# Four early loads of batch 0 issued by the scalar queue instead of the sync queue

## The chip, the core and the metric

The kernel runs on one core of a Trainium2 chip. The metric is the time of one execution on the device, in microseconds (us); smaller is better. Engines go by the short names of the profile: PE (TensorE, matmuls), PEld (its weight loads), DVE (VectorE), ACT (ScalarE), POOL (GpSimd) and SP (SyncE, which here only issues transfers). A name with a q behind it (SPq, ACTq, POOLq) is the instruction queue of that engine while it issues a transfer.

## What is computed

Attention with a forget gate, for 8 batches, 8 heads, 576 tokens and a head size of 64, is followed by a gated feed-forward layer over all 4608 tokens.

```
scores = q @ k.T / 8;  cum = cumsum(log(clip(f, 1e-4, 1)))
attn   = softmax(where(causal, -1e9, scores + cum[:, None] - cum[None, :]))
x      = (attn @ v)  with the heads side by side        # 4608 x 512
xn     = x / sqrt(mean(x*x) + 1e-6) * rms_g
out    = (silu(xn @ w_gate) * (xn @ w_val)) @ w_out     # 512 -> 1536 -> 512
```

All inputs and the output are float32 in device memory; the matmuls take bf16.

## The kernel before

**Work.** Batches are taken one after the other. For each, q, k and v are loaded as float32 into staging tiles `st` (a pool of 10), q and k are cast to bf16 (`ld`, a pool of 6) and turned so that the head dimension lies on partitions (tiles `QK`, and `QT` for the last 64 tokens). For batch 0 the turning is done by PE against an identity and a copy out of PSUM. Scores go to PSUM (L671), their exponentials to `PT` (L680, ACT), v is multiplied by the decay of its token and stored as `Vs` (L449 to L456), and values (L708), normalisation and the feed-forward layer follow (L857, L883), in groups of tokens that are mixed into the attention of later batches.

**Order.** Nothing is scheduled at run time. Each piece of work has a name, and the string ORDER (L22 to L102) lists all pieces; they are recorded in that order, so each engine's instruction queue has its own pieces in the order of the string. A suffix `@A`, `@D`, `@O` or `@S` puts a piece on ACT, DVE, POOL or SP instead of its default; `*48` puts that much filler matmul work ahead of a PE piece (L250); `:ff` picks a PSUM pool. The engines run their queues in order and meet by semaphores.

**The loads of batch 0.** Every load of q, k and v is issued by SP (`nc.sync.dma_start`). `Lk0.u` and `Lq0.u` load four heads and 256 tokens each (L459), 256 KB. `Lqk00` and `Lqk01` load the last 64 tokens of q and of k (L425), 128 KB each, into the lower and the upper 64 partitions of one staging tile. `Lv0.j` loads 128 tokens of v (L417), 256 KB in rows of 256 bytes; `Lv0.40` and `Lv0.41` load the last 64 tokens of v, the even and the odd heads (L429), 64 KB each. The one transfer that ACT issues early is `lf`, the forget gate (L272). The weights `wg0` to `wv3` (L382) and `wo` (L394) are issued by POOL.

SP's order in the first microseconds is Lk1.0, Lk0.0, Lk0.1, Lq0.0, Lq0.1, Lqk00, Lqk01, Lv0.40, Lk0.2, Lk0.3, Lq0.3, Lq0.2, Lv0.41, Lv0.1, Lv0.2, Lv0.0, Lv0.3, Lk1.2. Transfers of SP and ACT use eight completion semaphores in turn, so in the built program a transfer also waits for the landing of the one eight places before it in the order of the string.

**Who uses them.** ACT's order at the start is lf, fetch_ln (a table load and a small activation, L333), log (L280, needs clip on DVE, which needs lf), fetch (a second table load, L330), Cq0.0, Ck0.1 (casts, L223), expo (L292, needs the scan on DVE), keeptr0.02.k, keeptrt0, esc0.1.0 and so on. The first real work of PE is `tr0.01` (L535), which needs Ck0.0 on DVE and Cq0.0 on ACT; then come turn_rg, far0.1.0 and far0.3.0 (L659), eight units of filler, tr0.02 and tr0.03 (need Ck0.1 and Cq0.1), turn_dec (L302, needs expo and twice), trt0 (L553, needs Cqk0) and the first scores. On DVE, Cq0.1 and Cqk0 (both L223) stand behind twice (L295), which needs expo. POOL's order is Ck0.2, k4.0 (a copy that needs keeptrt0), Ck0.3, Cq0.2, Sv0.1, then the issues of the weights.

Of the kernel before, what the change touches and what calls it, by code (L numbers as in the profile page):

```python
# [11 lines left out]
ACT = mybir.ActivationFunctionType  # L12
PSUM = bass.MemoryType.PSUM

B, H, S, D = 8, 8, 576, 64
# [4 lines left out]
NP = H // 2  # L20

ORDER = """  # L22
one lf tri Lk1.0 Lk0.0 Lk0.1 far Lq0.0 ident Lq0.1 rg identb Lqk00 fetch_ln clip Lqk01 clear Lv0.40 log Lk0.2 Lk0.3 fetch Ck0.0@D scan Lq0.3 Lq0.2
Cq0.0@A Ck0.1@A Lv0.41 tr0.01*48 turn_rg far0.1.0 keeptr0.01.k@D expo Lv0.1 far0.3.0 keeptr0.01.q twice Cq0.1@D Cqk0@D tr0.02*8 Lv0.2 tr0.03
keeptr0.02.k@A keeptr0.02.q turn_dec Ck0.2@O keep_rgT keeptr0.03.k trt0 keeptr0.03.q sc0.1.0 keeptrt0@A keep_dec tr0.00 Lv0.0 esc0.1.0 sc0.3.0 k4.0
keeptr0.00.k far0.0.0*3 keeptr0.00.q@A Ck0.3@O Lv0.3 spread_rg Cq0.3@A Cq0.2 esc0.3.0 Sv0.4 tr0.10 Lk1.2 sc0.0.0 Lqk10 Sv0.1@O far0.2.0 esc0.0.0
keeptr0.10.k@D sc0.2.0 Lq1.2 esc0.2.0 Lq1.0 sc0.1.384*1 Sv0.2 tr0.12 wv1 esc0.1.384 Lqk11 sc4.0 keeptr0.12.k keeptr0.12.q Lk1.1 wg0 exp4.0 sc0.2.384*6
Lk1.3 keeptr0.10.q far0.3.1024 esc0.2.384 mask4.0 sc0.3.1024 Sv0.0 Lq1.1 far0.1.1024 wg1 esc0.3.1024 wv0 sc0.3.384*8 sc0.1.1024 esc0.3.384 wg2
val0.6.0 esc0.1.1024 Lq1.3 sc0.1.512 val0.0.0:ff wv2 val0.2.0:ff xpo0.0.0 esc0.1.512 sc0.2.512 Ck1.0 xpo0.2.0 val0.4.0:ff esc0.2.512 Sv0.3@O xpo0.6.0
# [76 lines left out]
ROWS, RUNS, HALF, TAIL, V4 = (1.2, 26, 64), (0.75, 46, 16), (0.9, 28, 32), (0.64, 24, 32), (0.34, 24, 16)  # L106
# [80 lines left out]
def kernel(  # L187
# [12 lines left out]
    nc = tc.nc  # L200
# [3 lines left out]
    def pool(name, bufs, **kw):  # L204
# [22 lines left out]
    ident = consts.tile([128, 128], BF16, name="ident")  # L227
    tri = consts.tile([128, 64], BF16, name="tri")
# [38 lines left out]
    clear = plan.add("clear", "DVE", 1.75, clear_early)  # L267
# [6 lines left out]
    lf = plan.add("lf", "ACT", 0.65, load_f, xfer=(0.4, 84, 4), acq=[("pt", "pre")])  # L274
# [39 lines left out]
    far = consts.tile([128, 256], BF16, name="far")  # L314
# [91 lines left out]
    def attention(b):  # L406
        i = b % 2
        old, new = hist.get(b - 2, {}), hist.setdefault(b, {})
        split, pe = b in SPLIT, b in PE_TURN
        cold = COLD if b == 0 else 1  # L410

        def stage(key):
            if key not in T:
                T[key] = stp.tile([128, H * D], F32, name="st", tag="st")
            return T[key]

        def load_rows(nm, src, j):  # L417
            nc.sync.dma_start(out=stage((nm + "s", b, j)).rearrange("p (h d) -> p h d", d=D),
                              in_=src[b, :, j * 128:(j + 1) * 128, :].rearrange("h p d -> p h d"))

        def load_runs(nm, src, pp):
            nc.sync.dma_start(out=stage((nm + "s", b, pp)).rearrange("p (h c) -> p h c", h=2),  # L422
                              in_=src[b, 2 * pp:2 * pp + 2, 0:512, :].rearrange("h (p i) d -> p h (i d)", i=4))

        def load_tail(t, src):  # L425
            nc.sync.dma_start(out=stage(("qks", b))[t * 64:t * 64 + 64, :].rearrange("p (h d) -> p h d", d=D),  # L426
                              in_=src[b, :, 512:576, :].rearrange("h p d -> p h d"))

        def load_v4(par):  # L429
            nc.sync.dma_start(out=stage(("vs", b, 4))[par * 64:par * 64 + 64, 0:NP * D].rearrange("p (h d) -> p h d", d=D),  # L430
                              in_=v[b, par::2, 512:576, :].rearrange("h p d -> p h d"))

        def cast(src, dst, eng, runs=False):
# [22 lines left out]
                e.tensor_copy(Vs[i][rows, 4, par::2, D], dj)  # L456

        ld, lv, sv, tq = {}, {}, {}, {}
        def load_half(nm, src, u):  # L459
            hh, z = divmod(u, 2)  # L460
            nc.sync.dma_start(out=stage((nm + "s", b, u)).rearrange("p (h c) -> p h c", h=4),
                              in_=src[b, 4 * z:4 * z + 4, hh * 256:hh * 256 + 256, :].rearrange("h (p i) d -> p h (i d)", i=2))

        def load_qk(us):
            for u in us:
                for nm, src in (("k", k), ("q", q)):
                    key = f"{nm}{b}.{u}"
                    if split:
                        a = [plan.add("L" + key, "SP", 0.65, lambda nm=nm, src=src, u=u: load_half(nm, src, u), xfer=HALF,
                                      acq=[("st", "s" + key)])]  # L470
                        eng = SPLIT_CAST[u][nm]
                    else:
                        fn = load_runs if pe else load_rows
                        a = [plan.add("L" + key, "SP", 0.6 if pe else 0.66, lambda fn=fn, nm=nm, src=src, u=u: fn(nm, src, u),
                                      xfer=RUNS if pe else ROWS, acq=[("st", "s" + key)])]
                        eng = CAST_ON.get((nm, b, u), "POOL")
                    eng = on("C" + key, eng)
                    ld[nm, u] = plan.add("C" + key, eng, {"DVE": 0.45, "ACT": 0.6, "POOL": 0.62}[eng],
                                         lambda nm=nm, u=u, eng=eng: cast((nm + "s", b, u), (nm, b, u), eng, pe), a,
                                         acq=[("ld", key)], rel=["s" + key])  # L480

        def load_tails():
            key = f"qk{b}"
            a = [plan.add(f"L{key}{t}", "SP", 0.66, lambda t=t, src=src: load_tail(t, src), xfer=TAIL,
                          acq=[("st", "s" + key)])
                 for t, src in enumerate((q, k))]
            eng = on("C" + key, "POOL")
            ld["t"] = plan.add("C" + key, eng, 0.62, lambda: cast(("qks", b), ("qk", b), eng), a,
                               acq=[("ld", key)], rel=["s" + key])

        def load_v(js):
            for j in js:
                key = f"v{b}.{j}"
                if j < 4:
                    lv[j] = [plan.add("L" + key, "SP", 0.66, lambda j=j: load_rows("v", v, j), acq=[("st", "s" + key)],
                                      xfer=ROWS)]
                else:
                    lv[j] = [plan.add(f"L{key}{par}", "SP", 0.66, lambda par=par: load_v4(par),
                                      acq=[("st", "s" + key)], xfer=V4) for par in range(2)]
                eng = on("S" + key, "DVE" if b == 0 else SV_ON.get((b, j), "POOL"))  # L500
                sv[j] = plan.add("S" + key, eng, (0.82 if j < 2 else 1.0 if j < 4 else 1.6) if eng == "DVE" else 1.25 if j < 4 else 1.7, lambda j=j, eng=eng: scale_v(j, eng),
                                 lv[j] + [p_dec, clear] + old.get("val", []), rel=["s" + key])
# [12 lines left out]
        if pe:  # L515
# [444 lines left out]
```

## Time and profile before

| | |
|---|---|
| median of 6 runs | 384.1 us (383.68 to 384.99) |
| the profiled execution | 384.56 us |
| its span, first to last instruction | 382.8 us |
| outside the span | 1.8 us |
| PE busy | 369.2 us, 96% of the span |
| DVE, ACT, POOL busy | 265.8, 220.4, 127.3 us |
| transfers issued by SP (q1) | 40.00 MB, 52.8% of 16 DMA engines |
| transfers issued by POOL (q0) | 8.79 MB, 10.8% |
| transfers issued by ACT (q10) | 3.29 MB, 2.5% |

The page cuts the span into 40 slices of 9.6 us. PE is at 50% in the first slice, between 80% and 90% in the four behind it and nearly full from then on. The clock granted to PE is 0.8 of full speed in the first slice, 0.5 in the second, and full from the third to the end. The DMA engines are busy over 90% in the first seven slices. So the first 48 us hold most of what PE is not yet doing, and the change lies within the first 20.

### The profile page before, as it was taken

To read this page: it belongs to the slowest core of one execution; us is meant where nothing else is said; L and a number is where in the kernel's file an instruction comes from. 1 tells how busy PE (TensorE), PEld (TensorE's weight loads), DVE (VectorE), ACT (ScalarE), POOL (GpSimd) and SP (SyncE) were. 2 spreads that over 40 slices of the span, in tenths; PEclk is the share of its full clock that TensorE was granted. 3 is DMA by queue.
4 is the path that set the end of the run, shared out by engine and by line. 5 is a ranking of instruction groups with operands and counts; after the bars stand their busy time and mean duration, and the time that the engine had idled before them with its cause. 6 is when DMAs were issued, how large, how long until landed. Compare 5 with 4: busy or idle time off the path is not lost.

```text
span 382.8 us, 8265 instructions
## 1 busy us (share of the span) xinstructions
PE 369.2 (96%) x3212; PEld 198.5 (52%) x3212; DVE 265.8 (69%) x502; ACT 220.4 (58%) x369; POOL 127.3 (33%) x190
## 2 busy tenths in 40 slices
PE   5988899998999999999999999999999999999996
PEld 2656678654554544454445445454445544444443
DVE  5576787699786578668756877498556965754661
ACT  5588864875768768645775576446465353331310
POOL 3583494253364244632421476130311110000101
PEclk8599999999999999999999999999999999999999
DMA  9999999297997899998967992632120024001203
GB/s 205 252 251 198 211 198 241 66 216 146 191 204 166 176 204 172 251 156 182 206 145 138 208 221 43 149 93 36 41 70 30 14 57 110 1 8 48 82 2 110
DMA packets 145831, 52.60 MB, mean 137 GB/s; under 512 B 128220, under 2 KB 142176, under 8 KB 145792
## 3 DMA queue, kind: packets, MB, share of 16 engines
q1 hardware_dynamic: 136912, 40.00, 52.8%
q0 software_dynamic: 7072, 8.79, 10.8%
q10 hardware_dynamic: 1808, 3.29, 2.5%
q8 instruction: 25, 0.41, 0.5%
q14 instruction: 14, 0.11, 0.2%
HBM read 37.90 MB, written 9.44 MB: 124 GB/s over the span
## 4 chain that ended last, share of the span: by engine, by line
PE 77%; issue 6%; POOL 5%; DMA 4%; DVE 3%; ACT 2%; SPq 1%; POOLq 0%; ACTq 0%; DVEq 0%
PE ff L857 43%; PE ff L883 23%; PE sc L671 5%; PE po L708 4%; DMA st<-in_q_dram 4%; PE ff L708 2%; POOL ld L223 2%; ACT PT L680 1%; DVE xn L733 1%; POOL wg L382 1%; SPq L422 1%; SPq L426 1%; POOL Vs L449 1%; DVE ga L866 1%; POOL rs L729 1%
## 5 line engine op out<-in xcount | busy, mean ns | idle before, releaser
L680 ACT ACTIVATE PT<-sc 128x1024 bf16<-128x1024 f32 (+2 forms) x100 | 96.0, 992 | 31.9 <-PE sc L671 30.8
L862 ACT ACTIVATE th<-ff 128x512 f32<-128x512 f32 x108 | 64.5, 597 | 84.2 <-PE ff L857 78.0
L857 PE MATMUL ff<-xT,wv 128*128 128x512 bf16 (+1 forms) x480 | 111.1, 358 | 1.2 <-DVE hT L873 0.6
L857 PE MATMUL ff<-xT,wg 128*128 128x512 bf16 (+1 forms) x480 | 111.1, 358 | 1.1 <-DVE hT L873 1.1
L866 DVE SCALAR_TENSOR_TENSOR ga<-th,ff 128x512 f32<-128x512 f32 x108 | 73.9, 685 | 44.2 <-ACT th L862 43.6
L883 PE MATMUL ff<-wo,hT 128*128 128x512 bf16 (+1 forms) x444 | 99.2, 374 | 0.0
L873 DVE SCALAR_TENSOR_TENSOR hT<-ga,ff 128x512 bf16<-128x512 f32 x108 | 73.9, 685 | 9.5 <-PE ff L857 2.1
L857 PEld LDWEIGHTS <-wg 128*128 128x128 bf16 x480 | 45.0, 98 | 44.0 <-issue 2.8
L857 PEld LDWEIGHTS <-wv 128*128 128x128 bf16 x480 | 44.6, 98 | 43.5 <-issue 3.7
L883 PEld LDWEIGHTS <-hT 128*128 128x128 bf16 x444 | 42.3, 98 | 47.3 <-issue 1.5
L688 POOL TENSOR_SCALAR_AFFINE_SELECT PT<-PT 128x1024 bf16<-128x1024 bf16 x28 | 33.6, 1201 | 88.2 <-ACT PT L680 84.1
L733 DVE SCALAR_TENSOR_TENSOR xn<-X,rs,rgb 128x512 bf16<-128x512 f32 x40 | 35.1, 900 | 10.1 <-POOL rs L729 10.1
L708 PEld LDWEIGHTS <-PT 128*128 128x128 bf16 x896 | 33.8, 98 | 10.9 <-DVE X L716 1.3
L891 POOL DMA_DIRECT2D out_dram<-ores x16 | 9.4, 589 | 69.0 <-ACT ores L223 36.8
L671 PE MATMUL sc<-QK 64*128 64x128 bf16 (+2 forms) x328 | 28.8, 273 | 0.0
L449 POOL TENSOR_TENSOR Vs<-st,decT 128x512 bf16<-128x512 f32 x21 | 22.0, 1048 | 17.5 <-DMA st<-in_v_dram 12.8
L223 ACT COPY ores<-ff 128x512 f32<-128x512 f32 (+1 forms) x19 | 10.9, 576 | 28.3 <-PE ff L883 28.3
L723 ACT ACTIVATE junk<-X 128x513 bf16<-128x513 f32 x40 | 25.4, 636 | 1.6 <-DVE X L716 1.0
L708 PE MATMUL po<-Vs,PT 128*128 128x65 bf16 x599 | 25.5, 194 | 0.2 <-DVE Vs L450 0.2
L729 POOL TENSOR_TENSOR rs<-sq,mhalf 128x5 f32<-128x5 f32 (+2 forms) x9 | 10.1, 1125 | 46.7 <-ACT junk L723 46.7
L223 POOL CAST ld<-st 128x512 bf16<-128x512 f32 x31 | 20.3, 673 | 13.4 <-DMA st<-in_k_dram 11.0
L671 PEld LDWEIGHTS <-QK 64*128 64x128 bf16 x584 | 15.3, 95 | 17.5 <-issue 13.9
(90 smaller groups left out, 271.7 us busy)
## 6 DMA issues: line engine op xcount, KB each, us to landing
st<-in_k_dram SPq DMA_DIRECT2D x32, 256.0 KB, 4.0
st<-in_q_dram SPq DMA_DIRECT2D x32, 256.0 KB, 4.9
st<-in_v_dram SPq DMA_DIRECT2D x32, 256.0 KB, 4.5
out_dram<-ores POOLq DMA_DIRECT2D x15, 256.0 KB, 3.1
out_dram<-ores ACTq DMA_DIRECT2D x12, 256.0 KB, 2.6
out_dram<-ores SPq DMA_DIRECT2D x8, 256.0 KB, 2.3
wo<-in_moe_w_out_dram POOLq DMA_DIRECT2D x2, 768.0 KB, 13.6
st<-in_q_dram SPq DMA_DIRECT2D x8, 128.0 KB, 5.1
```

Of the source, the lines that this page charges most:

```text
L223: {"DVE": nc.vector.tensor_copy, "POOL": nc.gpsimd.tensor_copy, "ACT": nc.scalar.copy}[eng](o, x)
L449: e.tensor_tensor(Vs[i][:, j, :, 0:D], t, bcast(dj, D), ALU.mult)
L671: nc.tensor.matmul(sc[:, par, c:c + n], lhsT=k_cols(r, p, kj), rhs=q_cols(r, p, q0, n), start=not opened, stop=not opened or (kj, q0) == b ...
L680: nc.scalar.activation(T["pt", b, p][:, :, c0:c0 + n], T.pop(("sc", b, p, c0))[:, :, 0:n], ACT.Exp, scale=scale)
L688: nc.gpsimd.affine_select(out=d, in_=d, pattern=[[0, m], [1, 128]], compare_op=ALU.is_ge, fill=0.0, base=0, channel_multiplier=-1)
L708: nc.tensor.matmul(T["po", b, hs][:, qm, m, :], lhsT=w, rhs=Vs[i][:, kj, h, :], start=(kj == 0), stop=(kj == qi))
L733: nc.vector.scalar_tensor_tensor(xn, in0=X[i][:, j, 0:DM], scalar=T["rs", b, js][:, j:j + 1], in1=rgb, op0=ALU.mult, op1=ALU.mult)
L857: nc.tensor.matmul(ps[:, c * w:c * w + w], lhsT=wt[:, dc, (fc + c) * 128:(fc + c + 1) * 128], rhs=T["xT", g][:, dc, 0:w], start=(dc == 0), ...
L862: nc.scalar.activation(t, T["pg", g, fc], ACT.Tanh, scale=0.5)
L866: nc.vector.scalar_tensor_tensor(a, in0=T.pop(("th", g, fc)), scalar=1.0, in1=T.pop(("pg", g, fc)), op0=ALU.add, op1=ALU.mult)
L873: nc.vector.scalar_tensor_tensor(o, in0=T.pop(("ga", g, fc)).rearrange("p (c t) -> p c t", t=w), scalar=0.5, in1=T.pop(("pv", g, fc)).rear ...
L883: nc.tensor.matmul(po, lhsT=T["hT", g][:, fc, j * 128:(j + 1) * 128], rhs=wo[:, fc, c0:c1], start=(fc == 0), stop=(fc == NFC - 1))
```

## The change

ORDER marks four loads of batch 0 with `@A`, and the load functions take the engine that issues them. Nothing else in the string moves: no piece changes place, size or tile.

```
-... Lqk00 fetch_ln clip Lqk01 clear Lv0.40 log ...
+... Lqk00 fetch_ln clip Lqk01@A clear Lv0.40 log ...
-Cq0.0@A Ck0.1@A Lv0.41 ... expo Lv0.1 far0.3.0 ...
+Cq0.0@A Ck0.1@A Lv0.41@A ... expo Lv0.1@A far0.3.0 ...
-... keeptr0.00.q@A Ck0.3@O Lv0.3 spread_rg Cq0.3@A ...
+... keeptr0.00.q@A Ck0.3@O Lv0.3@A spread_rg Cq0.3@A ...

+        def ring(eng):
+            return nc.scalar if eng == "ACT" else nc.sync
-        def load_tail(t, src):
-            nc.sync.dma_start(out=stage(("qks", b))[...], ...)
+        def load_tail(t, src, eng):
+            ring(eng).dma_start(out=stage(("qks", b))[...], ...)
...
-            a = [plan.add(f"L{key}{t}", "SP", 0.66, ...
+            a = [plan.add(f"L{key}{t}", on(f"L{key}{t}", "SP"), 0.66, ...
```

`load_rows`, `load_runs`, `load_half` and `load_v4` are changed in the same way as `load_tail`. In ACT's instruction queue the four issues stand so: Lqk01 behind fetch_ln and ahead of log; Lv0.41 behind Ck0.1 and ahead of expo; Lv0.1 behind expo and ahead of keeptr0.02.k; Lv0.3 behind keeptr0.00.q and ahead of Cq0.3. In SP's queue the four are missing, and what stood behind them moves up.

More of the change, by code (lines that the diff above doesn't have):

```diff
@@ L22 @@
 ORDER = """
-one lf tri Lk1.0 Lk0.0 Lk0.1 far Lq0.0 ident Lq0.1 rg identb Lqk00 fetch_ln clip Lqk01 clear Lv0.40 log Lk0.2 Lk0.3 fetch Ck0.0@D scan Lq0.3 Lq0.2
-Cq0.0@A Ck0.1@A Lv0.41 tr0.01*48 turn_rg far0.1.0 keeptr0.01.k@D expo Lv0.1 far0.3.0 keeptr0.01.q twice Cq0.1@D Cqk0@D tr0.02*8 Lv0.2 tr0.03
+one lf tri Lk1.0 Lk0.0 Lk0.1 far Lq0.0 ident Lq0.1 rg identb Lqk00 fetch_ln clip Lqk01@A clear Lv0.40 log Lk0.2 Lk0.3 fetch Ck0.0@D scan Lq0.3 Lq0.2
+Cq0.0@A Ck0.1@A Lv0.41@A tr0.01*48 turn_rg far0.1.0 keeptr0.01.k@D expo Lv0.1@A far0.3.0 keeptr0.01.q twice Cq0.1@D Cqk0@D tr0.02*8 Lv0.2 tr0.03
 keeptr0.02.k@A keeptr0.02.q turn_dec Ck0.2@O keep_rgT keeptr0.03.k trt0 keeptr0.03.q sc0.1.0 keeptrt0@A keep_dec tr0.00 Lv0.0 esc0.1.0 sc0.3.0 k4.0
-keeptr0.00.k far0.0.0*3 keeptr0.00.q@A Ck0.3@O Lv0.3 spread_rg Cq0.3@A Cq0.2 esc0.3.0 Sv0.4 tr0.10 Lk1.2 sc0.0.0 Lqk10 Sv0.1@O far0.2.0 esc0.0.0
+keeptr0.00.k far0.0.0*3 keeptr0.00.q@A Ck0.3@O Lv0.3@A spread_rg Cq0.3@A Cq0.2 esc0.3.0 Sv0.4 tr0.10 Lk1.2 sc0.0.0 Lqk10 Sv0.1@O far0.2.0 esc0.0.0
 keeptr0.10.k@D sc0.2.0 Lq1.2 esc0.2.0 Lq1.0 sc0.1.384*1 Sv0.2 tr0.12 wv1 esc0.1.384 Lqk11 sc4.0 keeptr0.12.k keeptr0.12.q Lk1.1 wg0 exp4.0 sc0.2.384*6
@@ L415, in stage, with load_rows, load_runs, load_v4 @@
             return T[key]
-        def load_rows(nm, src, j):
-            nc.sync.dma_start(out=stage((nm + "s", b, j)).rearrange("p (h d) -> p h d", d=D),
+        def ring(eng):
+            return nc.scalar if eng == "ACT" else nc.sync
+        def load_rows(nm, src, j, eng):
+            ring(eng).dma_start(out=stage((nm + "s", b, j)).rearrange("p (h d) -> p h d", d=D),
                               in_=src[b, :, j * 128:(j + 1) * 128, :].rearrange("h p d -> p h d"))
-        def load_runs(nm, src, pp):
-            nc.sync.dma_start(out=stage((nm + "s", b, pp)).rearrange("p (h c) -> p h c", h=2),
+        def load_runs(nm, src, pp, eng):
+            ring(eng).dma_start(out=stage((nm + "s", b, pp)).rearrange("p (h c) -> p h c", h=2),
                               in_=src[b, 2 * pp:2 * pp + 2, 0:512, :].rearrange("h (p i) d -> p h (i d)", i=4))
-        def load_tail(t, src):
-            nc.sync.dma_start(out=stage(("qks", b))[t * 64:t * 64 + 64, :].rearrange("p (h d) -> p h d", d=D),
+        def load_tail(t, src, eng):
+            ring(eng).dma_start(out=stage(("qks", b))[t * 64:t * 64 + 64, :].rearrange("p (h d) -> p h d", d=D),
                               in_=src[b, :, 512:576, :].rearrange("h p d -> p h d"))
-        def load_v4(par):
-            nc.sync.dma_start(out=stage(("vs", b, 4))[par * 64:par * 64 + 64, 0:NP * D].rearrange("p (h d) -> p h d", d=D),
+        def load_v4(par, eng):
+            ring(eng).dma_start(out=stage(("vs", b, 4))[par * 64:par * 64 + 64, 0:NP * D].rearrange("p (h d) -> p h d", d=D),
                               in_=v[b, par::2, 512:576, :].rearrange("h p d -> p h d"))
@@ L458, in attention, with load_half @@
         ld, lv, sv, tq = {}, {}, {}, {}
-        def load_half(nm, src, u):
+        def load_half(nm, src, u, eng):
             hh, z = divmod(u, 2)
-            nc.sync.dma_start(out=stage((nm + "s", b, u)).rearrange("p (h c) -> p h c", h=4),
+            ring(eng).dma_start(out=stage((nm + "s", b, u)).rearrange("p (h c) -> p h c", h=4),
                               in_=src[b, 4 * z:4 * z + 4, hh * 256:hh * 256 + 256, :].rearrange("h (p i) d -> p h (i d)", i=2))
@@ L468, in load_qk @@
                     if split:
-                        a = [plan.add("L" + key, "SP", 0.65, lambda nm=nm, src=src, u=u: load_half(nm, src, u), xfer=HALF,
+                        lq = on("L" + key, "SP")
+                        a = [plan.add("L" + key, lq, 0.65, lambda nm=nm, src=src, u=u, lq=lq: load_half(nm, src, u, lq), xfer=HALF,
                                       acq=[("st", "s" + key)])]
@@ L473, in load_qk @@
                         fn = load_runs if pe else load_rows
-                        a = [plan.add("L" + key, "SP", 0.6 if pe else 0.66, lambda fn=fn, nm=nm, src=src, u=u: fn(nm, src, u),
+                        lq = on("L" + key, "SP")
+                        a = [plan.add("L" + key, lq, 0.6 if pe else 0.66, lambda fn=fn, nm=nm, src=src, u=u, lq=lq: fn(nm, src, u, lq),
                                       xfer=RUNS if pe else ROWS, acq=[("st", "s" + key)])]
@@ L483, in load_tails @@
             key = f"qk{b}"
-            a = [plan.add(f"L{key}{t}", "SP", 0.66, lambda t=t, src=src: load_tail(t, src), xfer=TAIL,
+            a = [plan.add(f"L{key}{t}", on(f"L{key}{t}", "SP"), 0.66, lambda t=t, src=src: load_tail(t, src, on(f"L{key}{t}", "SP")), xfer=TAIL,
                           acq=[("st", "s" + key)])
@@ L494, in load_v @@
                 if j < 4:
-                    lv[j] = [plan.add("L" + key, "SP", 0.66, lambda j=j: load_rows("v", v, j), acq=[("st", "s" + key)],
+                    lq = on("L" + key, "SP")
+                    lv[j] = [plan.add("L" + key, lq, 0.66, lambda j=j, lq=lq: load_rows("v", v, j, lq), acq=[("st", "s" + key)],
                                       xfer=ROWS)]
                 else:
-                    lv[j] = [plan.add(f"L{key}{par}", "SP", 0.66, lambda par=par: load_v4(par),
+                    lv[j] = [plan.add(f"L{key}{par}", on(f"L{key}{par}", "SP"), 0.66, lambda par=par, key=key: load_v4(par, on(f"L{key}{par}", "SP")),
                                       acq=[("st", "s" + key)], xfer=V4) for par in range(2)]
```

## Prediction

> **What bounds the kernel now.** I read the page first: PE is busy for 369.2 of 382.8 us, so the time is PE's work plus the places where PE stands idle or runs slowly. Its clock row says where the latter is.
>
> ```profile
> PE   5988899998999999999999999999999999999996
> PEclk8599999999999999999999999999999999999999
> DMA  9999999297997899998967992632120024001203
> ```
>
> All four moved loads lie in the first two slices. The waits between 17 and 40 us and between 40 and 75 us have no row that names a DMA, so from 17 us to 75 us nothing stands still for a transfer: whatever PE gains or loses before 17 us is carried on, unless slack takes it up. The question is thus what decides when PE gets through its first work. The timeline of PE, 0 to 10 us (columns: start, us, engine, line, operation, count, and in brackets the idle time before it with its releaser):
>
> ```profile
> 1.09 4.16 PE L254 MATMUL ff<-idle 128*128 128x512 bf16 x12 [1.09 <-DVE idle L266]
> 8.00 0.61 PE L535 MATMUL ff<-ident,ld 128*128 128x128 bf16 x4 [2.75 <-ACT ld L223]
> ```
>
> PE's first real work starts at 8.00, after 2.75 us without work, released by a cast on ACT, Cq0.0. ACT's timeline says what that cast waited for:
>
> ```profile
> 2.69 0.20 ACT L333 ACTIVATE warm<-one 64x1 f32<-64x1 f32 x1
> 5.07 0.68 ACT L280 ACTIVATE PT<-PT 64x576 f32<-64x576 f32 x1 [2.18 <-DVE PT L277]
> ...
> 7.06 0.20 ACT L330 ACTIVATE warm<-one 64x1 f32<-64x1 f32 x1
> 7.33 1.14 ACT L223 CAST ld<-st 128x512 bf16<-128x512 f32 x2
> 8.85 0.78 ACT L292 ACTIVATE PT<-PT,mid 64x576 f32<-64x576 f32 x1 [0.38 <-DVE mid L288]
> ```
>
> ACT is free for Cq0.0 at 7.26. The timeline of SP gives Lq0.0's issue, and the DMA view of a window that holds only that q issue, 2.3 to 2.9 us, gives 4.9 us from issue to landing (last column):
>
> ```profile
> 2.37 1.06 SPq L461 DMA_DIRECT2D st<-in_q_dram  x2
> 3.47 0.81 SPq L426 DMA_DIRECT2D st<-in_q_dram  x1
> 4.33 0.84 SPq L426 DMA_DIRECT2D st<-in_k_dram  x1
> ```
>
> ```profile
> st<-in_q_dram SPq DMA_DIRECT2D x1, 256.0 KB, 4.9
> ```
>
> 2.37 + 4.9 = 7.3: the cast starts when Lq0.0 has landed. There is **no slack** on that landing. The same view of other windows gives 5.4 us for Lq0.1 (issued at 2.88, lands at 8.3), 5.6 for Lqk00 (lands at 9.1) and 5.4 for Lqk01 (lands at 9.7), one after the other. SP issues in 0.5 to 0.85 us what lands every 0.7 to 1.1 us, and the DMA row is at 9 throughout: the engines that move bytes set the landings, not SP's issuing.
>
> **The change, part by part.**
>
> *Lqk01 to ACT.* On ACT the issue comes right behind fetch_ln, at 2.9 us, with no wait of its own. ACT is idle until 5.07 there (2.18 us), so an issue of 0.6 to 0.85 us (SP's own 64-row issues) costs ACT nothing; log does not move. But the transfer now has a queue of its own, and no longer stands behind Lq0.0 and Lq0.1. What two queues do to each other is seen at 34 to 42 us, where POOL's weights and SP's loads run together (DMA view of that window: queue, packets, MB, share):
>
> ```profile
> q0 software_dynamic: 1247, 1.24, 91.1%
> q1 hardware_dynamic: 1247, 0.32, 29.9%
> ```
>
> Both moved exactly 1247 packets: they take turns packet by packet, whatever the size. Lqk01 has 512 packets of 256 bytes; Lk0.1 and Lq0.0 have 512 of 512 bytes each. The first transfers on idle queues landed 2.9 us (SP) and 3.7 us (ACT's lf) after their issue at 0.81, so at 2.9 + 2.9 to 2.9 + 3.7 Lqk01 would land alone, at 5.8 to 6.6; taking turns makes it later, but most of its packets pass ahead of the end of Lq0.0. Price: Lqk01's landing is now 9.7 - 9.1, some 0.7 us behind Lqk00's; so **Lq0.0 lands up to 0.7 us later**. The low end is 0, if ACT's packets only come once Lq0.0 is through; a rate gives 128 KB at 291 GB/s (window 5 to 7 us), 0.45. I take 0.7, the landing step of this very transfer.
>
> The Trainium skill has the same turns between queues ("DMA: Bandwidth & Descriptors", Queues, rings and completion order), but of the purpose of such a change it says that starting transfers from several engines saves only sequencer time ("Issuing engines are not separate DMA queues"). By that rule alone the move is worth at most SP's 0.84 us and harms nothing; by the rows above SP's time is worth nothing and Lq0.0 pays.
>
> *Lv0.41 to ACT.* It stands between Ck0.1 and expo, and waits for the landing of Lq0.1. Casts: 7.33 + 0.7 to 8.47 + 0.7 = 9.17; Lq0.1 at 8.3 + 0.7 = 9.0, so no wait. The issue costs 0.81 by SP's row for it (its sister took 1.17, the shortest of four 0.61), less the 0.38 us in which ACT had waited for mid. Expo thus starts at 9.17 + 0.81 = 9.98 instead of 8.85, ends at 10.75, and twice, Cq0.1 and Cqk0 on DVE follow it. Cq0.1 ended near 10.2 in the old profile and now ends near 11.3. PE reaches tr0.02, which needs it, at 10.84 + 0.7 = 11.54, because its filler and far_first pieces come first. So the issue is hidden, with 0.2 us to spare; with 1.17 us, 0.1 us shows. I take **0.1**; the ends are 0 and 0.4.
>
> *Lv0.1 to ACT.* It stands behind expo. ACT was idle 1.89 us from 9.63 to 11.51, and in the new order from 10.75 to 12.2. The issue took 0.55 to 1.5 us on SP among the v loads at 10.04 to 14.89. Hidden, just, in its longest case. keeptr0.02.k is behind it, and PE's scores wait for that.
>
> *Lv0.3 to ACT.* It stands ahead of Cq0.3 and esc0.3.0, which ended at 16.26. Far0.2.0 on PE (17.70) needs the PSUM that esc0.3.0 frees: slack 1.4 us, and ACT has 1.55 us of idle time before 17.82. An issue of 0.55 to 1.5 us is hidden or nearly so.
>
> *SP without the four.* It loses 0.84 + 0.81 and two of the four v issues in 4.85 us, some 4 us of queue time. The bytes are the same and the DMA engines are full, so landings only change places. Lv0.41 and Lv0.1 pass Lq0.3 and Lq0.2; Lq0.2 (8.5 + 5.5 = 14.0) can land up to 0.4 + 0.95 later, at 15.4. Its cast on POOL comes at 15.4, now 0.7 later. Hidden. Ck0.2 is the one load on which POOL really waits:
>
> ```profile
> 10.99 0.60 POOL L223 CAST ld<-st 128x512 bf16<-128x512 f32 x1 [7.02 <-DMA st<-in_k_dram]
> 13.85 0.87 POOL L223 COPY K<-QT 64x256 bf16<-64x256 bf16 x2 [2.26 <-ACT QT L223]
> ```
>
> If Lk0.2 lands sooner, POOL's next piece still waits 2.26 us for ACT, which hangs on PE's tr0.02 and trt0. DVE's wait of 0.4 us for Lv0.41 at 14.42 goes; next DVE waits 1.92 us for PE at 17.42. Neither is worth anything.
>
> **Sum.** 0.7 + 0.1 = **+0.8 us**, carried to the end. Against the profiled execution that is 382.8 + 0.8 of span and 1.8 around it, 385.4 in all; this execution was 0.46 over the median of the runs shown, so against the median 384.1 the forecast is **384.9**. What may shrink it is the clock (the table of windows cut where the granted clock changes; columns: us, then busy us and count of PE, PEld, DVE, ACT, POOL, then clock, DMA share, GB/s):
>
> ```profile
> 7.37:10.78 3.41, 2.78 (x15) 1.83 (x16) 2.83 (x8) 1.88 (x3) 0.00 (x0) 0.50 1.29 235
> 10.78:14.19 3.41, 3.41 (x28) 2.34 (x28) 2.06 (x7) 1.35 (x3) 0.94 (x2) 0.50 1.27 260
> 14.19:17.61 3.42, 3.42 (x27) 2.55 (x25) 1.27 (x3) 2.08 (x5) 3.30 (x7) 0.50 1.36 219
> 17.61:21.02 3.41, 3.02 (x42) 1.92 (x40) 2.04 (x5) 3.05 (x6) 1.56 (x3) 1.00 1.20 245
> ```
>
> PE is full from 10.78 to 17.61 at half clock. If the full clock returns at the same moment, 0.7 us of half-speed work moves behind it and takes 0.35 there, if PE alone sets the pace. But DVE, ACT and POOL keep their speed, and from 18.7 on PE waits for them repeatedly; I keep 0.7, with 0.35 as the low end.
>
> The Trainium skill ("TensorE: Matmul & The Clock Gate", The HAM clock gate) says that one busy window of about 3.4 us releases the full clock. By it the clock would have been back at 14.19, after 3.41 of 3.41 us busy; the row has 0.50 for one more window. By the rule the 0.7 us would fall in a stretch that ends sooner; by the row it doesn't.
>
> **Rivals.**
>
> 1. *The shift is hidden.* ACT's packets come late, or the clock and slack take the shift up: 0 to +0.3 us, 384.1 to 384.4. For it: lf landed 0.8 us later than SP's transfer issued at the same time, and ACT's queue may lag more with SP's issues ahead. Against it: Lqk01 has 4.4 us until 7.3.
>
> 2. *Slower by more: the full clock returns one window later,* at 21.02. PE's 3.02 busy us of 17.61 to 21.02 then take up to twice as long at their matmuls, say half of it more, 1.5: up to 0.8 + 1.5, 385.3 to 386.4. For it: PE starts 0.7 us later, and 2.78 of 3.41 was not enough in an earlier window. Against it: PE stays full from 10.78 + 0.7 on. ACT's issues taking over 1.5 us each would end in the same range.
>
> 3. *Faster: the full clock returns one window sooner,* at 14.19, since other pieces now fall in the window that decides. 3.42 busy us at half clock would take 1.7 less, and 0.8 is lost: -0.9, 383.2; 382.4 to 383.3. It decides as soon as the window from 10.8 to 14.2 is counted as busy. For it: that window was full and yet had no effect, so what is in it matters. Against it: a later start puts more turns (L535) and fewer scores (L671) there.
>
> The program does do what it says: its ACT queue holds the four issues.
>
> **Chances.** About 0.2%, 0.8 us, is what a measurement of this kernel can tell from no change. Forecast, 384.5 to 385.3: 0.54 (0.34 above 384.87, 0.20 below). Rival 1: 0.11, within. Rival 2: 0.19, slower. Rival 3: 0.16, faster. Together: faster 0.16, same 0.31, slower 0.53. The range reaches half into rival 3 and most of the way into rival 2: 383.0 to 386.2. It holds 0 and 0.7 for the transfer and 0 to 0.4 for expo.
>
> **What would show it.** In the new profile: ACTq with an issue of `st<-in_k_dram` at 2.9 us, and ACT's Cq0.0 and PE's first L535 near 8.0 and 8.7 instead of 7.33 and 8.00 (transfer); expo near 10.0 instead of 8.85, and no idle time of PE before tr0.02 that names DVE (Lv0.41); no idle time of PE at far0.2.0 that names ACT beyond the old 0.2 us (Lv0.3); the full clock still from 17.6. If Cq0.0 stays at 7.33, the first term is wrong; if the first L535 moves by 0.7 and the end doesn't, the carrying is.

## The result, and the profile after

| | before | after |
|---|---|---|
| median of all runs beside each other | 384.12 us (48 runs) | 385.54 us (24 runs, 384.94 to 387.69) |
| ratio | | 1.0041 [1.0031, 1.0051] |
| the profiled execution | 384.56 us | 387.14 us |
| its span | 382.8 us | 385.4 us |

The kernel became slower by 1.4 us between the medians, 1.6 us by the ratio. The forecast was +0.8. The execution of the new kernel that was profiled is one of its slowest, 1.6 us above its own median, while the one of before is 0.4 us above; so the profile below shows the mechanism larger than it is in most executions (2.6 us instead of 1.4), and its sizes are compared with other profiles further down. In the new kernel the lines behind L416 have moved: turns are L541 (was L535), far pieces L665 (L659), scores L677 (L671), and the loads L425, L429, L433 and L464 (L422, L426, L430 and L461).

The page's second part, its rows for PE, PE's clock and the DMA engines (40 slices):

```profile
PE   5888899998999999999999999999999999999996
PEclk9599999999999999999999999999999999999999
DMA  9999999398999979989957993634120024001202
```

PE has lost in the second slice (8 instead of 9) and nothing is new behind it, so I read the timeline of PE at the start (start, us, engine, line, operation, count, idle time before with its releaser):

```profile
1.09 5.17 PE L254 MATMUL ff<-idle 128*128 128x512 bf16 x12 [1.09 <-DVE idle L266]
9.21 0.47 PE L541 MATMUL ff<-ident,ld 128*128 128x128 bf16 x4 [2.96 <-ACT ld L223]
10.69 0.24 PE L358 MATMUL ff<-ident_f,rg 4*128 4x4 f32 x1 [1.01 <-DMA rg<-in_moe_rms_g_dram]
10.86 1.46 PE L665 MATMUL sc<-far,ident 128*128 128x256 bf16 x8
```

The first turn comes at 9.21, 1.21 us later than before. Then a second wait has appeared: turn_rg, which followed at once before (8.54), now waits 1.01 us for the 2 KB of rms_g that POOL loads. At 10.69 PE is 2.15 us behind, and stays there: the first gate matmuls (L863) start at 39.01 instead of 36.92, 2.09 us later. The chain of waits of this execution has that small load as one of its longest pieces (start, us, what):

```profile
3.30 7.26 DMA rg<-in_moe_rms_g_dram
```

ACT's timeline:

```profile
1.41 1.28 ACT L333 ACT_TABLE_LOAD   x1 [1.41 <-PEq L950]
1.47 0.71 ACTq L429 DMA_DIRECT2D st<-in_k_dram  x1
2.70 0.20 ACT L333 ACTIVATE warm<-one 64x1 f32<-64x1 f32 x1
5.60 0.68 ACT L280 ACTIVATE PT<-PT 64x576 f32<-64x576 f32 x1 [2.70 <-DVE PT L277]
...
8.54 1.14 ACT L223 CAST ld<-st 128x512 bf16<-128x512 f32 x2 [0.74 <-DMA st<-in_q_dram]
10.18 0.60 ACTq L433 DMA_DIRECT2D st<-in_v_dram  x1
10.89 0.78 ACT L292 ACTIVATE PT<-PT,mid 64x576 f32<-64x576 f32 x1 [1.21 <-DVE QK L223]
10.97 0.47 ACTq L421 DMA_DIRECT2D st<-in_v_dram  x1
```

Lqk01 is issued at **1.47, not at 2.9**: the table load ahead of it (1.41 to 2.69) doesn't hold the issue back, which starts while it runs. The same is seen at 10.97, where Lv0.1 is issued while expo runs. Cq0.0 now waits visibly for q, 0.74 us, and starts at 8.54 instead of 7.33; even the log is later (5.60 instead of 5.07), since lf lands later. The DMA view of windows that hold one issue each, 2.3 to 2.9 us (Lq0.0) and 1.45 to 1.48 us (Lqk01; last column: us from issue to landing):

```profile
st<-in_q_dram SPq DMA_DIRECT2D x1, 256.0 KB, 6.1
```

```profile
st<-in_k_dram ACTq DMA_DIRECT2D x1, 128.0 KB, 5.8
```

Lq0.0, issued at 2.37 as before, lands at 8.5 instead of 7.3. Lqk01 lands at 1.47 + 5.8 = 7.3, ahead of it, where before it came 2.5 us behind it.

What the queues moved between 3.95 and 7.37 us is in the DMA view of that window (queue, packets, MB, busy share). Before:

```profile
q1 hardware_dynamic: 2045, 0.97, 119.3%
```

After:

```profile
q1 hardware_dynamic: 1294, 0.65, 98.6%
q10 hardware_dynamic: 531, 0.13, 20.8%
```

ACT's queue moved Lqk01's 0.13 MB, but SP's queue moved 0.32 MB less. So in this execution ACT's packets took the place of SP's bytes, and the sum was lower as well, 227 GB/s for 283. A shorter window shows how uneven it was. From 5.0 to 5.5 us of after:

```profile
q10 hardware_dynamic: 274, 0.07, 69.2%
q1 hardware_dynamic: 94, 0.04, 42.6%
```

ACT's queue moved three packets to one of SP's there, and from 4.5 to 6.0 us 486 to 406. By 6.5 us all of Lqk01's packets were through, when SP's queue had moved 0.74 MB, less than the 0.79 MB of the three loads ahead of Lq0.0.

The windows cut where the granted clock changes (columns as in the prediction's table):

```profile
9.41:12.82 3.41, 2.40 (x15) 1.52 (x13) 1.61 (x5) 1.05 (x2) 0.91 (x1) 0.50 1.23 248
12.82:16.24 3.42, 3.42 (x28) 2.26 (x28) 2.13 (x8) 1.28 (x3) 0.47 (x2) 0.50 1.32 235
16.24:19.65 3.41, 3.41 (x28) 2.63 (x27) 0.83 (x3) 2.16 (x5) 3.29 (x7) 0.50 1.27 244
19.65:23.06 3.41, 3.08 (x40) 1.88 (x36) 2.08 (x5) 3.09 (x6) 1.61 (x3) 1.00 1.13 223
```

The half clock lasts three windows, 9.41 to 19.65, as it did before (7.37 to 17.61). So it lies 2.04 us later and is not longer. PE's start doesn't explain where it lies: the filler ahead of all turns already took 5.17 us for 4.16 (first rows of PE's timelines), and in other profiles the half clock sets in at 7.16 to 10.46 us without following the first turn (v only, below: 9.30, with the first turn at 7.94).

### The profile page after: what moved, and what is told of

Its sections match the earlier page's. It is cut to its first block, busy times and chain, and to the rows that moved or that the text cites. A ratio compares the mean times of both kernels' runs of the same rounds, so it can differ in the third digit from the quotient of the medians.

```text
span 385.4 us, 8265 instructions
## 1 busy us (share of the span) xinstructions
PE 370.2 (96%) x3212; PEld 198.5 (52%) x3212; DVE 265.4 (69%) x502; ACT 220.6 (57%) x369; POOL 127.5 (33%) x190
## 4 chain that ended last, share of the span: by engine, by line
PE 78%; POOL 8%; issue 5%; DVE 4%; ACT 2%; DMA 2%; POOLq 0%; ACTq 0%; DVEq 0%
PE ff L863 42%; PE ff L889 23%; PE sc L677 5%; PE po L714 4%; DMA rg<-in_moe_rms_g_dram 2%; PE ff L714 2%; POOL Vs L452 2%; POOL ld L223 2%; ACT PT L686 1%; DVE xn L739 1%; POOL PT L694 1%; PE ff L254 1%; POOL wg L382 1%; POOL wv L382 1%; DVE Vs L453 1%
## 5 line engine op out<-in xcount | busy, mean ns | idle before, releaser
L863 PE MATMUL ff<-xT,wv 128*128 128x512 bf16 (+1 forms) x480 | 111.1, 358 | 1.4 <-DVE hT L879 0.6
L863 PE MATMUL ff<-xT,wg 128*128 128x512 bf16 (+1 forms) x480 | 111.1, 358 | 1.1 <-DVE hT L879 1.1
L863 PEld LDWEIGHTS <-wg 128*128 128x128 bf16 x480 | 44.9, 98 | 44.0 <-issue 2.8
L863 PEld LDWEIGHTS <-wv 128*128 128x128 bf16 x480 | 44.6, 98 | 43.6 <-issue 3.9
L677 PE MATMUL sc<-QK 64*128 64x128 bf16 (+2 forms) x328 | 28.7, 272 | 0.0
L677 PEld LDWEIGHTS <-QK 64*128 64x128 bf16 x584 | 15.3, 95 | 17.5 <-issue 13.9
```

The source lines that it names most:

```text
L677: nc.tensor.matmul(sc[:, par, c:c + n], lhsT=k_cols(r, p, kj), rhs=q_cols(r, p, q0, n), start=not opened, stop=not opened or (kj, q0) == b ...
L863: nc.tensor.matmul(ps[:, c * w:c * w + w], lhsT=wt[:, dc, (fc + c) * 128:(fc + c + 1) * 128], rhs=T["xT", g][:, dc, 0:w], start=(dc == 0), ...
```

## Experiments

The theory that the prediction holds (A): Lqk01's packets in a second queue delay Lq0.0, and PE's start is carried to the end. Its rivals: the three v issues on ACT are what costs; or the new wait for rms_g is part of the loss (C). Short names of the runs are explained where they come. This table gives what each execution that was profiled showed (landing of Lq0.0, start of the first turn, start of the first far piece behind turn_rg), its own time, and the kernel's median and ratio to before:

| kernel | Lq0.0 lands | first turn | far piece | its time | median | ratio |
|---|---|---|---|---|---|---|
| before | 7.31 | 8.00 | 8.74 | 384.56 | 384.1 | |
| after | 8.52 | 9.21 | 10.86 | 387.14 | 385.54 | 1.0041 [1.0031, 1.0051] |
| tail only | 8.13 | 8.83 | 9.78 | 385.06 | 385.49 | 1.0033 [1.0017, 1.0049] |
| v only | 7.25 | 7.94 | 8.82 | 384.79 | 384.68 | 1.0017 [1.0001, 1.0033] |
| v again | 7.20 | 7.93 | 8.84 | 386.13 | 384.47 | 1.0017 [0.9998, 1.0037] |
| rg first | 7.74 | 8.44 | 9.18 | 384.70 | 385.49 | 1.0042 [1.0022, 1.0063] |
| tail late | 7.48 | 9.36 | 10.09 | 385.65 | 385.49 | 1.0043 [1.0026, 1.0060] |
| half dose | 8.52 | 9.22 | 9.95 | 386.02 | 384.73 | 1.0025 [1.0008, 1.0042] |
| q01 ring | 8.45 | 9.14 | 9.67 | 384.32 | 385.43 | 1.0039 [1.0022, 1.0057] |
| q00 ring | 7.38 | 8.98 | 10.32 | 385.65 | 385.09 | 1.0031 [1.0011, 1.0051] |
| k10 late | 6.83 | 7.55 | 9.21 | 384.42 | 384.25 | 1.0008 [0.9992, 1.0024] |
| k10 rg | 6.75 | 7.47 | 8.28 | 382.83 | 383.27 | 0.9987 [0.9972, 1.0002] |
| k10 rg cq | 6.45 | 7.17 | 7.94 | 382.46 | 382.96 | 0.9981 [0.9967, 0.9995] |

**Tail only:** Lqk01 on ACT, the three v loads back on SP.

```
-... Lv0.41@A ...  Lv0.1@A ...  Lv0.3@A
+... Lv0.41   ...  Lv0.1   ...  Lv0.3
```

> Only the k half of the last 64 tokens goes to ACT; the three v loads are back on SP. Theory A (this one transfer, in a queue of its own, holds up the landing of Lq0.0 and of everything near it): the whole loss is here, +1.4 us against before (1.0037, as the changed kernel's 1.0041), Cq0.0 on ACT well behind 7.33 us, PE's first turn (L535 of before) about a microsecond behind 8.00. Theory B (the v issues on ACT hold expo and the exponentials): under 0.4 us is left (1.001 or less).

Measured: 1.0033 [1.0017, 1.0049], a median of 385.49, next to the whole change's 385.54. PE's timeline:

```profile
8.83 0.61 PE L541 MATMUL ff<-ident,ld 128*128 128x128 bf16 x4 [3.14 <-ACT ld L223]
9.61 0.24 PE L358 MATMUL ff<-ident_f,rg 4*128 4x4 f32 x1 [0.17 <-DMA rg<-in_moe_rms_g_dram]
9.78 1.46 PE L665 MATMUL sc<-far,ident 128*128 128x256 bf16 x8
```

The first turn is 0.83 us late, like Lq0.0's landing (8.13 for 7.31), and the wait for rms_g is only 0.17. By the medians Lqk01 alone makes most of the loss or all of it.

**V only:** the other part, Lqk01 back on SP and the three v loads on ACT.

```
-... Lqk01@A ...
+... Lqk01   ...
```

> Only the three v loads are issued by ACT; the k half of the last 64 tokens is back on SP. Theory A: nothing in front of Lq0.0 has changed, so Cq0.0 at 7.3 us, PE's first turn at 8.0 us and a time within 0.2 us of before (0.9995 to 1.0005); expo starts up to 0.8 us later but PE's filler covers it. Theory B: +0.8 to +1.4 us (1.002 to 1.004).

Measured: 1.0017 [1.0001, 1.0033]. Nothing is late at the start: the first turn comes at 7.94. Its profiled execution lost 0.9 us near 130 us, far behind the change, where DVE waited:

```profile
129.33 0.69 DVE L223 COPY ores<-ff 128x512 f32<-128x512 f32 x1 [2.88 <-DMA out_dram<-ores]
```

It waited for the landing of a store of the output that ACT had issued, where the execution of before that was profiled waited for PE. One execution can't tell whether that is the rule; the kernel was run once more, below.

**Rg first:** the whole change, with the load of rms_g issued first by POOL, to take C's wait away.

```
-one lf tri ... Lq0.1 rg identb ...
+one lf rg tri ... Lq0.1 identb ...
```

> The changed kernel, with POOL issuing the 2 KB load of rms_g first of all its work instead of at 3.3 us. In the changed kernel's profile PE waits 1.01 us for that load behind its first turn. Theory C (that wait is part of the loss): the wait goes, and the time falls by 0.5 to 1.0 us against the changed kernel (1.0015 to 1.003 against before). If only Lq0.0 counts: the wait goes, but its place is taken by PE's next one, and the time stays at 1.004.

Measured: 1.0042 [1.0022, 1.0063]; no gain. The load now lands at 5.7 us and PE doesn't wait for it:

```profile
8.44 0.61 PE L541 MATMUL ff<-ident,ld 128*128 128x128 bf16 x4 [3.19 <-ACT ld L223]
8.98 0.27 PE L358 MATMUL ff<-ident_f,rg 4*128 4x4 f32 x1
```

So C isn't seen in the median, though the 1.01 us in the profile of after is real for that execution. The interval leaves room for a gain of up to 0.7 us.

**Tail late:** Lqk01 on ACT, but behind the log, so that its packets come behind Lq0.0's.

```
-... clip Lqk01@A clear Lv0.40 log Lk0.2 ...
+... clip clear Lv0.40 log Lqk01@A Lk0.2 ...
```

> The changed kernel, with the k half still issued by ACT but behind log, so at about 5.1 to 5.8 us instead of 1.5 us, when Lq0.0's packets are mostly through. Theory A: Lq0.0 lands near 7.3 us again, PE starts near 8.0 us, and the time is within 0.4 us of before (1.000 to 1.001). If instead a second queue costs something wherever it runs beside the first: +0.7 us or more (1.002 and above).

Measured: 1.0043 [1.0026, 1.0060], not what was expected. Lq0.0 did land early, at 7.48, but ACT's timeline shows a new wait:

```profile
6.58 0.69 ACTq L429 DMA_DIRECT2D st<-in_k_dram  x1
7.30 1.28 ACT L330 ACT_TABLE_LOAD   x1 [1.37 <-DMA st<-in_k_dram]
...
8.70 0.60 ACT L223 CAST ld<-st 128x512 bf16<-128x512 f32 x1
```

The issue itself had to wait for the landing of Lk0.1 at 6.56, whose completion semaphore it was given, and the table load behind it in ACT's queue waited with it. (By eight places in the order of the string it would have been lf, which landed at 4.73; the transfers of the built program don't all stand in that order.) Cq0.0 came at 8.70 although its data had been there for 1.2 us. So this run doesn't separate the transfer's place from the issue; it shows that a late start of PE costs about as much when a held ACT makes it late.

**Half dose:** of all four only another, smaller load stands on ACT: Lv0.40, 64 KB in packets of 256 bytes, issued at 1.47.

```
-... Lqk01@A clear Lv0.40 ...    (Lv0.41, Lv0.1, Lv0.3 back on SP)
+... Lqk01 clear Lv0.40@A ...
```

> In place of the k half of the last 64 tokens (128 KB, 512 packets), Lv0.40 (64 KB, 256 packets) is issued by ACT at the same point, 1.5 us; all else is on SP. Theory A by bytes (each packet that passes in the second queue delays Lq0.0 by its own time): half of the loss, +0.5 to +0.8 us (1.0013 to 1.002), PE's first turn at 8.3 to 8.5 us. If a second queue costs a fixed amount whatever it carries: +1.4 us as before (1.0035). If only a transfer of 128 KB or more reaches Lq0.0: within 0.2 us of before.

Measured: 1.0025 [1.0008, 1.0042]; the median is 0.73 above before's 384.0, half of the tail's 1.41. The intervals overlap, so "half" is what the medians say, not more. Its profiled execution (386.02) is 1.3 us above its median, and shows no smaller delay of Lq0.0 than after's (8.52 in both). So a delay in proportion to the bytes isn't shown.

**Q01 ring:** Lq0.1, 256 KB in 512-byte packets over all partitions, on ACT; nothing else.

```
-... ident Lq0.1 rg ... Lqk01@A ...
+... ident Lq0.1@A rg ... Lqk01 ...
```

> In place of the k half, Lq0.1 (256 KB, 512 packets of 512 bytes to all 128 partitions), which is not needed before 9.8 us, is issued by ACT right behind lf; all else is on SP. Theory A by bytes: Lq0.0 lands 0.9 to 1.2 us later than 7.3, so PE's first turn near 9 us and +0.9 to +1.4 us (1.0025 to 1.0037). If the loss comes from the short rows or from writing one half of the partitions: the packets of Lq0.1 cost less, and the time is within 0.5 us of before.

Measured: 1.0039 [1.0022, 1.0057]. Lq0.1 lands at 6.52 and Lq0.0 at 8.45, the first turn is at 9.14. The delay is thus not a matter of Lqk01's short packets or its 64 partitions: all three transfers that passed Lq0.0 in a second queue did it. But 256 KB cost no more than Lqk01's 128 KB (+1.43 and +1.41 between the medians). Whether the same load would cost as much if it stood ahead of Lq0.0 in SP's own queue was not run. The nearest are the three k10 kernels below, which take 256 KB out from ahead of Lq0.0 in that queue: it lands 0.48 to 0.86 us earlier.

**K10 late:** if the landing of Lq0.0 sets the time, pulling it ahead must gain. No load but lf stands on ACT; Lk1.0, the first transfer of SP, goes behind Lqk01, and Cq0.0 goes to POOL, which is free.

```
-one lf tri Lk1.0 Lk0.0 ... Lqk01@A clear ...  Cq0.0@A
+one lf tri Lk0.0 ... Lqk01 Lk1.0 clear ...    Cq0.0@O
```

> No load on ACT's queue but lf. The load of batch 1 that SP issues first of all (Lk1.0, 256 KB) goes behind the last 64 tokens of batch 0, and Cq0.0 is cast by POOL, which is idle then, since ACT is not free before 7.26 us. Theory A (PE starts when Lq0.0 has landed, and a shift there is carried to the end): Lq0.0 lands at about 6.4 us, PE's first turn at 7.2 us (Ck0.0 on DVE ends at 7.1), and the time is 0.5 to 0.8 us below before (0.998 to 0.9987). If the start isn't what is carried: 1.000.

Measured: 1.0008 [0.9992, 1.0024]. PE's timeline says why:

```profile
7.55 0.57 PE L541 MATMUL ff<-ident,ld 128*128 128x128 bf16 x4 [1.64 <-POOL ld L223]
9.01 0.26 PE L358 MATMUL ff<-ident_f,rg 4*128 4x4 f32 x1 [0.90 <-DMA rg<-in_moe_rms_g_dram]
```

The first turn is 0.45 us earlier than before, but the next wait, for rms_g, took its place: turn_rg is later than before (8.54).

**Q00 ring:** Lq0.0 itself on ACT, issued at 1.40 instead of 2.37, and Cq0.0 on POOL.

```
-... far Lq0.0 ident ... Lqk01@A ...   Cq0.0@A
+... far Lq0.0@A ident ... Lqk01 ...   Cq0.0@O
```

> The transfer that PE waits for, Lq0.0, is itself issued by ACT right behind lf, and cast by POOL; all else is on SP. If queues take turns, Lq0.0 passes the others: it lands at 5.8 to 6.6 us, PE starts at 7.2 to 7.5 us, and the time is 0.3 to 0.8 us below before (0.998 to 0.9992). If a second queue slows all transfers alike, Lq0.0 lands at 7.3 us or later and the time is 0 to 1 us above before (1.000 to 1.0026).

Measured: 1.0031 [1.0011, 1.0051]. The DMA view of the window 1.35 to 1.45 us has the row of its issue:

```profile
st<-in_q_dram ACTq DMA_DIRECT2D x1, 256.0 KB, 6.0
```

1.40 + 6.0 = 7.4: issued 1 us earlier, it lands no earlier than before (7.3), and Lk0.1 (7.90 for 6.43) and rms_g (10.08 for 8.36) land later. The second queue delayed others and didn't bring the landing of its own transfer forward. The time of this run is not the queue's alone, though. The first turn comes at 8.98, 1.6 us behind the landing, since POOL's cast took 1.48 us:

```profile
7.44 1.48 POOL L223 CAST ld<-st 128x512 bf16<-128x512 f32 x1 [3.46 <-DMA st<-in_q_dram]
```

DVE's scan ran beside it (7.17 to 8.51). In k10 late the same cast takes 0.60. So 0.9 us of the late first turn come from POOL's slower cast, which the edit brought with it.

**V again:** the same kernel as v only, to see whether its loss holds.

> The kernel of the run with only the three v loads on ACT once more, since its interval (1.0001 to 1.0033) leaves open whether they cost anything, and its profiled execution had lost 1.0 us at 130 us, where a cast out of PSUM waited for a store to land. Theory A: they cost nothing, within 0.3 us of before (0.9995 to 1.0008), and the profile has no shift behind 20 us that isn't there at 9 us. Theory B: +0.6 us or more again (1.0015 and above).

Measured: 1.0017 [0.9998, 1.0037], as in the first series. Nothing is late at the start (first turn 7.93, far piece 8.84), and PE is within 0.2 us of before up to 69 us. At 130 us DVE waits as in the first profile of this kernel, for the same store:

```profile
130.39 0.69 DVE L223 COPY ores<-ff 128x512 f32<-128x512 f32 x1 [2.69 <-DMA out_dram<-ores]
```

Across this wait ACT's instructions fall back by 0.9 us against before in both profiles of this kernel (from 1.0 early to 0.1 early in v only, from 0.3 to 1.2 late here). The store took 4.9 and 4.7 us to land; in the other eleven profiles it took 3.3 to 4.1, and DVE waited for PE at this place. So both profiles place a loss of 0.9 us, 110 us behind the moved loads. Part of the median's goes with the clock: 6 of these 24 executions have a mean granted clock below 0.9885, against 2 of the 98 of before that ran beside the experiments, and at the highest clocks (0.9935 and more) the medians differ only by 0.4 (384.25 for 383.83) and 0.1 us (383.83 for 383.69), which speaks against a wait of 0.9 us in every execution. **Why the store lands later there, and in how many executions, stays open.**

**K10 rg:** before's loads, with both edits: Lk1.0 behind Lqk01 and Cq0.0 on POOL, and the load of rms_g first.

> Lk1.0 issued behind the last 64 tokens of batch 0 and Cq0.0 cast by POOL, as in the run before, and besides POOL issues the load of rms_g first of all: in the run before, PE started at 7.55 us and then waited 0.90 us for it. Theory A: that wait goes, PE comes to tr0.02 some 0.8 us sooner than before's 10.84 us or as soon as Cq0.1 is cast, and the time is 0.3 to 0.8 us below before (0.998 to 0.9992). If the wait is only passed on to the next one (Cq0.1 behind twice on DVE): 1.000.

Measured: 0.9987 [0.9972, 1.0002]. No wait for rms_g is left, and the next one shows in PE's timeline, Cq0.1 on DVE:

```profile
7.47 0.68 PE L535 MATMUL ff<-ident,ld 128*128 128x128 bf16 x4 [2.32 <-POOL ld L223]
8.08 0.26 PE L358 MATMUL ff<-ident_f,rg 4*128 4x4 f32 x1
...
10.81 0.62 PE L535 MATMUL ff<-ident,ld 128*128 128x128 bf16 x8 [0.22 <-DVE ld L223]
```

**K10 rg cq:** the same, and Cq0.1 on POOL too.

```
-... twice Cq0.1@D Cqk0@D ...
+... twice Cq0.1@O Cqk0@D ...
```

> The same, and Cq0.1 is cast by POOL too, so that it no longer stands behind twice, and so behind the forget gate's chain, on DVE. Theory A: PE runs without a wait from its first turn to tr0.02; 0.6 to 1.0 us below before (0.9975 to 0.9985). If the next wait (turn_dec for expo, or the casts of trt0) takes its place: no better than the run with Cq0.1 on DVE.

Measured: 0.9981 [0.9967, 0.9995], 382.96 us, which beats both kernels. PE's timeline, then its windows:

```profile
7.17 0.64 PE L535 MATMUL ff<-ident,ld 128*128 128x128 bf16 x4 [1.84 <-POOL ld L223]
7.74 0.26 PE L358 MATMUL ff<-ident_f,rg 4*128 4x4 f32 x1
7.94 1.46 PE L659 MATMUL sc<-far,ident 128*128 128x256 bf16 x8
9.19 1.06 PE L254 MATMUL ff<-idle 128*128 128x512 bf16 x2
10.05 1.04 PE L535 MATMUL ff<-ident,ld 128*128 128x128 bf16 x8
```

```profile
7.53:10.94 3.41, 3.41 (x21) 2.31 (x21) 2.84 (x7) 1.45 (x3) 1.56 (x2) 0.50 1.20 261
10.94:14.36 3.42, 2.85 (x34) 2.07 (x32) 2.65 (x8) 2.49 (x7) 2.17 (x5) 1.00 1.28 257
```

The first far piece is 0.80 us earlier than before and the median 1.0 us lower. PE is full from 7.17 on, and here the half clock lasts one window only.

## Why the prediction was half right

**What bounds the start: right.** Lq0.0's landing has no slack. In after, tail only and q01 ring the first turn moves with that landing: by 1.21, 0.83 and 1.14 us for landings 1.21, 0.82 and 1.14 us later. In the table the time of an execution follows its far piece, once executions with the same number of half-clock windows (below) are compared. With three windows, far pieces at 8.74, 9.95 and 10.86 go with 384.56, 386.02 and 387.14 us (before, half dose, after); with two, 9.18, 9.78, 10.09 and 10.32 with 384.70, 385.06, 385.65 and 385.65 (rg first, tail only, tail late, q00 ring); with one, 7.94, 8.28, 9.21 and 9.67 with 382.46, 382.83, 384.42 and 384.32 (k10 rg cq, k10 rg, k10 late, q01 ring). Only v only and v again lie above these, by some 1.0 and 1.4 us, and they have the wait at 130 us.

**The step that failed is the first term of the sum, "Lq0.0 lands up to 0.7 us later", taken as the price of the whole move of Lqk01:** the mechanism holds, the size does not. By the ratio of tail only Lqk01 alone costs 1.3 us, 0.7 to 1.9. The landing itself was priced about right: against 7.31, the three profiles with Lqk01 on ACT early (after, tail only, rg first) have Lq0.0 1.21, 0.82 and 0.43 later, 0.82 in the mean. Nor is that the scatter of the first landing: Lq0.0 lands 3.2 to 3.6 us behind SP's first transfer in before, v only, v again and tail late, and 3.9 to 4.4 behind it in after, tail only, rg first, half dose and q01 ring. What came on top stands behind the landing: the first far piece is 2.12, 1.04 and 0.44 later, 1.2 in the mean.

Three things were wrong in the term. The issue was put at 2.9, behind ACT's table load, but came at 1.47; so in after all of Lqk01's packets went beside Lk0.0 and Lk0.1, ahead of Lq0.0, and not only most of them ahead of its end. I priced the bytes that pass ahead at an unchanged rate, but SP's queue moved 0.25 MB less between 3.95 and 7.37 us in tail only (0.72 for 0.97), for 0.13 MB of Lqk01's; some 0.05 MB of it is the first transfer's landing 0.18 us later there (3.91 for 3.73) at 283 GB/s. And the next wait, rms_g, wasn't asked for: POOL's 2 KB load landed at 8.36 before, 0.18 us ahead of its use, so whatever slowed all transfers could bring it out; it did by 1.01 and 0.17 us in two profiles. How the 1.3 us is shared out among these is not settled: with that wait taken away (rg first) the median stayed.

The measured 385.54 lies in the stated range, but above the forecast's own band (384.5 to 385.3) and in that of rival 2 (385.3 to 386.4), though not for rival 2's reason: the half clock has three windows in the profile of before and in that of after. The range reached that far for the sake of the clock, so that it held the result is in part luck.

The Trainium skill ("DMA: Bandwidth & Descriptors", Queues, rings and completion order) has each DMA engine change between queues packet by packet, and the prediction read such turns between POOL's queue and SP's from 34 to 42 us (1247 packets each). Between ACT's queue and SP's at the start the turns were not one for one (274 to 94 from 5.0 to 5.5 us in after; 259 to 34 in q01 ring); why is open. The skill's sentence that issuing from several engines saves only issue time ("Issuing engines are not separate DMA queues") would, taken alone, have given about 0 for tail only; the run has 1.0033.

**Lv0.41's 0.1 us: not seen, and not refuted.** In the profile of after the issue did wait, for Lq0.1's landing at 10.16 (I had 9.0), and expo came at 10.89 instead of the 9.98 worked out. PE didn't wait for it: at tr0.02 no idle time stands. But the v loads alone measure some 0.6 us that I had priced at 0.1 in all, and both of their profiles lose 0.9 us at the store near 130 us, a place that the prediction didn't look at; the profile of after doesn't have that wait. By the ratios the two parts sum to 1.0050 and the whole is 1.0041 with an upper end of 1.0051, so whether they add is open as well.

**SP's relief and Lv0.1, Lv0.3 at nothing: right as to the path.** POOL's cast Ck0.2 and the copy behind it, whose wait for ACT hid any gain:

```profile
11.91 1.11 POOL L223 CAST ld<-st 128x512 bf16<-128x512 f32 x1 [7.93 <-DVE PT L295]
15.98 0.96 POOL L223 COPY K<-QT 64x256 bf16<-64x256 bf16 x2 [2.95 <-ACT QT L223]
```

The copy still waits, 2.95 us now, and is late by PE's shift (15.98 for 13.85); no v load shortened it.

**The carrying: right.** 2.15 us at 10.7 and 2.09 us at 39.0 in the profile of after, and nothing hid it (rival 1).

**The clock (rivals 2 and 3): it changes by execution, not by kernel.** The half clock lasted one, two or three windows of 3.41 us in the various profiles: three in before, after, half dose and v again, two in tail only, rg first, tail late and q00 ring, one in the others. The mean granted clock of an execution tells which (0.9935 and more, then down to 0.9885, then less). At the highest, tail only has 385.42 and before 383.83 beside it, at the middle one 385.48 and 384.44. So the loss stands at equal clock, 1.6 and 1.0 us, and neither rival explains it. Rival 3's early clock did come, with better starts: all 12 executions of k10 rg cq and 11 of 12 of k10 rg are of the highest kind, against 19 of the 29 of before beside them. The Trainium skill ("TensorE: Matmul & The Clock Gate", The HAM clock gate) has one busy window release the clock; k10 rg cq agrees (3.41 of 3.41 us busy, then 1.00), the profiles of before and after do not (two such windows at 0.50).

## What to carry to other kernels

Before a load is given to a second queue, ask which landing the first real work waits for: with the DMA engines full, each of the three loads that passed it in a second queue delayed it (0.4 to 1.2 us for 64 to 256 KB, not in proportion), and a second queue didn't bring the landing of its own transfer forward (q00 ring). An issue on a compute engine is not only its own 0.6 us: it may come earlier than the program's order suggests (over a table load) or hold the engine by its own wait for an older transfer. To gain at a start-up, follow PE's waits one by one (q, then the small rms_g load, then the next cast): taking the first alone gained nothing that could be measured, the three together 1.0 us. And follow a shift or a loss through the whole profile: what both profiles of the v kernel lost stands 110 us behind its loads.

## What the runs showed of the hardware that was not expected

- ACT's instruction queue starts a DMA while the engine still works on what stands ahead of it: 1.47 us, with the table load from 1.41 to 2.69; 10.97, with expo from 10.89 to 11.67. A DMA that waits for a semaphore does hold ACT: 1.37 us without work in tail late, of which the issue itself is 0.69.
- Beside SP's queue, ACT's queue can get far more than every other packet: 274 to 94 from 5.0 to 5.5 us in after, where the rows of before from 34 to 42 us have 1247 each for POOL's queue and SP's.
- Between 3.95 and 7.37 us the DMA engines moved 227, 233, 251 and 274 GB/s with 256-byte packets in a second queue (after, half dose, tail only, rg first), 276 and 270 with 512-byte packets there (q01 and q00 ring), and 275 to 287 with SP's queue alone in the old order (before, the v kernels, tail late). But with SP's queue alone in the new order of the k10 kernels it is 252, 254 and 262. So a lower rate is not shown to come from the second queue.
- POOL's cast of 128x512 took 0.60 to 0.62 us for Cq0.0 and Ck0.2 in the k10 kernels, but 1.48 (Cq0.0 in q00 ring) and 1.55 (Cq0.1 in k10 rg cq) where DVE's scan ran beside it.
- A load of 2 KB issued by POOL took 5.1 us to land among SP's transfers (before), 7.3 in after, 4.3 when it was issued first (rg first).
- The first transfer on an idle queue, always issued at 0.81, landed at 3.7 to 4.3 us in different executions. That scatter is as large as many of the differences sought here, so a landing in one profile is better counted from the first landing than from the start.
